# X fills spread over the eight units of a row pair, and the row end's scaled rows formed on VectorE

## The chip, the cores and the metric

The kernel runs on one core of one Trainium2 chip. The metric is the device time of one launch in microseconds: the median of the runs, 1494.32 us before the change. Engines are named as in the profile: PE is TensorE's matmul row (PEld its weight loads), DVE is VectorE, ACT is ScalarE, POOL is GpSimd, SP is SyncE, which issues the DMAs.

## What is computed

The reference is the forward pass and the whole gradient of one E-Branchformer block: x is 2 x 4000 x 144 (bfloat16, K = 5 taps), and the outputs are the block's output and the gradients by x and by seven weights.

```python
qkv = einsum('btd,de->bte', layernorm(x), w_qkv)
p = softmax(einsum('btd,bsd->bts', q, k) * D ** (-0.5))
glob = einsum('btd,de->bte', einsum('bts,bsd->btd', p, v), w_att_out)
h = gelu(einsum('btd,de->bte', layernorm(x), w_mlp_in)); u, g = h[..., :D], h[..., D:]
gc = conv over t of layernorm(g) with dw_csgu
loc = einsum('btd,de->bte', u * gc, w_mlp_out)
m = concat([glob, loc]); m = m + conv over t of m with dw_merge
out = x + einsum('btc,cd->btd', m, w_merge)
# and jax.vjp of it all for grad_out
```

## The kernel before

For each of the two batches the kernel runs a head, an attention loop and a tail; the weights' gradients are finished at the end. The change lies in the attention loop, `phase_attn`. It holds the normalised x of one batch in SBUF, as rows (`xaa`) and transposed (`xaT`, with the 16 columns over 128 apart in `XR`), and for each of 32 blocks of 128 tokens a scaled query row block `Q_t` and its backward partner `B_t`.

**Rows and units.** The loop's index i is a row of 128 queries. A row is cut into four units c2 = 0 to 3 of 1000 keys; two rows, an even and an odd one, are a pair, so a pair has eight units, which this document numbers 0 to 7 (unit 0 is c2 = 0 of the even row). `unit(i, c2)` takes four PSUM tiles, two pS and two pD, from pools of two buffers each, and issues on PE four matmuls with 16 contracted rows (L1768, called XR here) and four with 128 (L1772, called XaT). ACT makes the exponentials Pm of pS (L1777), DVE the product Sm of pD and Pm (L1778), each in two halves, with the row sums as a by-product.

**The end of a row.** `row_end(i)` adds up the sums (ld, L1792), takes the reciprocal rl (L1794), and scales: nd and Qs on POOL (L1796, L1797), nr on POOL (L1799), br on ACT (L1801). `row_end2`, called inside the next row's first unit, between its two Sm, forms Bt = Qs nd + br on DVE (L1806). Qs and Bt have four buffers, Pm and Sm three rows.

**Two products of a finished row.** SP transposes Pm and Sm by DMA (`flip`), and two rows later `yz` multiplies them with xaa, a quarter of the row's work in each unit: 16 matmuls y (L1816); in the fourth quarter ACT copies y scaled (Q_t L1821, yd L1823) and DVE adds Zn (written over B_t, L1824). y has one PSUM buffer. `xfill(pr, f)` multiplies Sm and Pm of a pair's two rows with Qs and Bt: fill f, 0 to 10, covers three blocks of 128 keys with 12 matmuls X (L1833, L1834; the last fill has 8). Even fills are added to the accumulator acc by DVE straight from PSUM (L1841), odd ones are copied by ACT (xs, L1838) and added by POOL (L1839). X has two PSUM buffers.

**The order.** The loop is written in the order in which it runs (`manual_schedule`): each engine executes its instructions in the order of the code. Each unit has two places; the table `fills` says which fill stands at (unit, place), and before, a pair's fills ran during the following pair. At each place `Q.place()` also lets steps of the local branch run (convolutions, gelu, layer norm: tiles hs, sq, a_, h_t, gp_t, dgf, jk, dWs and others), which use one PSUM buffer (ps_f) and all engines.

Of the kernel before, what the change touches and what calls it, by code (L numbers as in the profile page):

```python
# [14 lines left out]
D = 144  # L15
# [1043 lines left out]
NBK = 32  # L1059
# [659 lines left out]
def phase_attn(k, W, b, S):  # L1719
    nc, tc = k.nc, k.tc  # L1720
    NP = 3
    GW = NBK * 128
    with ExitStack() as es:
        ab = es.enter_context(tc.tile_pool(name="at_buf", bufs=1))
        sm = es.enter_context(tc.tile_pool(name="at_sm", bufs=4))
# [31 lines left out]
        def unit(i, c2):  # L1757
            g, bi = divmod(i, 4)
            QTm, BTm, QBr = jt[g]
            pb = i % NP  # L1760
            if c2 == 0:
                st["ld", i] = sm.tile([128, 2, 8], F32, tag="ld8", name="ld8")
            ld8 = st["ld", i]
            pS = [ps_s.tile([128, 512], F32, tag="S", name="pS") for h in range(2)]
            pD = [ps_d.tile([128, 512], F32, tag="D", name="pD") for h in range(2)]
            for r, o_ in enumerate((pS[0], pD[0], pS[1], pD[1])):
                rr = slice(32 * r, 32 * r + DR)
                nc.tensor.matmul(o_[:, 0:SC], QBr[rr, bi, :], S.XR[rr, c2, 0:SC], start=True, stop=False)  # L1768
            c0 = 2 * c2 * SC
            for w_, p_ in ((QTm, pS), (BTm, pD)):  # L1770
                for h in range(2):
                    nc.tensor.matmul(p_[h][:, 0:SC], w_[:, bi, :], S.xaT[:, c0 + h * SC:c0 + (h + 1) * SC], start=False, stop=True)  # L1772
            with tc.high_priority():
                for h in range(2):
                    c1 = c0 + h * SC
                    n = 2 * c2 + h
                    nc.scalar.activation(P[:, pb, c1:c1 + SC], pS[h][:, 0:SC], ACT.Exp, accum_out=ld8[:, 0, n:n + 1])  # L1777
                    nc.vector.scalar_tensor_tensor(Sm[:, pb, c1:c1 + SC], pD[h][:, 0:SC], 1.0, P[:, pb, c1:c1 + SC], op0=ALU.mult, op1=ALU.mult,  # L1778
                                                   accum_out=ld8[:, 1, n:n + 1])
# [8 lines left out]
        def row_end(i):  # L1788
            pb = i % 4
            ld8 = st.pop(("ld", i))  # L1790
            ld = sm.tile([128, 2], F32, tag="ld")
            nc.vector.reduce_sum(ld[:], ld8[:], axis=AX.X)  # L1792
            rl = sm.tile([128, 1], F32, tag="rl", bufs=6)
            nc.vector.reciprocal(rl[:], ld[:, 0:1])  # L1794
            nd = sm.tile([128, 1], F32, tag="nd", bufs=6)
            nc.gpsimd.tensor_scalar(nd[:], ld[:, 1:2], rl[:], -1.0, op0=ALU.mult, op1=ALU.mult)  # L1796
            nc.gpsimd.tensor_scalar(Qs[:, pb, :], S.Q_t[:, i, :], rl[:], 1.0, op0=ALU.mult, op1=ALU.mult)  # L1797
# [3 lines left out]
            nc.scalar.activation(br[:], S.B_t[:, i, :], ACT.Copy, scale=rl[:])  # L1801
            st["rl", i], st["nr", i], st["nd", i], st["br", i] = rl, nr, nd, br

        def row_end2(i):
            pb = i % 4
            nc.vector.scalar_tensor_tensor(Bt[:, pb, :], Qs[:, pb, :], st.pop(("nd", i))[:], st.pop(("br", i))[:], op0=ALU.mult, op1=ALU.add)  # L1806

        def yz(i, part):
            if part == 0:
# [13 lines left out]
                nc.scalar.activation(yd[:], y[:, 0, :], ACT.Copy, scale=nr[:])  # L1823
                nc.vector.scalar_tensor_tensor(S.Zn[:, i, :], y[:, 1, :], rl[:], yd[:], op0=ALU.mult, op1=ALU.add)  # L1824

        def xfill(pr, f):
            j0 = f * 3
            nj = min(3, NBK - j0)
            X = ps_x.tile([128, 3, D], F32, tag="x", name="X")
            for jj in range(nj):  # L1830
                j = j0 + jj
                for kk, i in enumerate((2 * pr, 2 * pr + 1)):
                    nc.tensor.matmul(X[:, jj, :], Sm[:, i % NP, j * 128:(j + 1) * 128], Qs[:, i % 4, :], start=(kk == 0), stop=False)  # L1833
                    nc.tensor.matmul(X[:, jj, :], P[:, i % NP, j * 128:(j + 1) * 128], Bt[:, i % 4, :], start=False, stop=(kk == 1))  # L1834
            a_ = S.acc[:, j0:j0 + nj, :]
            if f % 2 == 1:
                xs = xp.tile([128, 3, D], F32, tag="xs", name="xs")
                nc.scalar.copy(xs[:, 0:nj, :], X[:, 0:nj, :])  # L1838
                nc.gpsimd.tensor_tensor(a_, xs[:, 0:nj, :], a_, op=ALU.add)  # L1839
            else:  # L1840
                nc.vector.tensor_tensor(a_, X[:, 0:nj, :], a_, op=ALU.add)  # L1841

        fills = {(1, 0): 0, (1, 1): 1, (2, 0): 2, (2, 1): 3, (3, 0): 4, (3, 1): 5, (4, 0): 6, (4, 1): 7, (5, 1): 8, (6, 0): 9, (6, 1): 10}
        Q = Steps()
        local_steps(k, W, b, S, es, ps_f, Q)
        with tc.manual_schedule():
            for _ in jit(0):
                pass  # L1850
# [468 lines left out]
```

## Time and profile before

| What | Value |
|---|---|
| median of 3 runs | 1494.32 us (1491.7 to 1496.08) |
| the profiled execution | 1494.56 us, span 1492.7 us |
| mean granted TensorE clock | 0.936 |
| attention loop, first batch | about 84 to 606 us of the span |
| attention loop, second batch | about 782 to 1324 us of the span |

The two stretches that the prediction tabulates, 160 to 640 us and 830 to 1325 us, lie nearly wholly in these loops. In a row of the timeline stand the start (us from the span's start), the duration, the engine, the line, and in brackets how long the engine had been idle and what ended that. A row of the waits names the waiting engine and line, what it waited for, the total in us, how often, and the longest. Matmul rows overlap each other, since PE is pipelined.

### The profile page before, as it was taken

To read this page: it belongs to the slowest core of one execution; us is meant where nothing else is said; L and a number is where in the kernel's file an instruction comes from. 1 tells how busy PE (TensorE), PEld (TensorE's weight loads), DVE (VectorE), ACT (ScalarE), POOL (GpSimd) and SP (SyncE) were. 2 spreads that over 40 slices of the span, in tenths; PEclk is the share of its full clock that TensorE was granted. 3 is DMA by queue.
4 is the path that set the end of the run, shared out by engine and by line. 5 is a ranking of instruction groups with operands and counts; after the bars stand their busy time and mean duration, and the time that the engine had idled before them with its cause. 6 is when DMAs were issued, how large, how long until landed. Compare 5 with 4: busy or idle time off the path is not lost. (4 is left out here: it accounts for less than half of the span.)

```text
span 1492.7 us, 40175 instructions
## 1 busy us (share of the span) xinstructions
PE 1318.6 (88%) x15366; PEld 989.9 (66%) x15366; DVE 890.4 (60%) x3021; ACT 829.3 (56%) x2441; POOL 572.9 (38%) x1065
## 2 busy tenths in 40 slices
PE   5989999999999999889679999999999999979932
PEld 3727767776676777789553767767776677679811
DVE  5535667677666666456334577667667666635442
ACT  3746666565666665354365666666666665435310
POOL 2224435344344443355232444444434443235400
PEclk9959999999999999999895999999999999999955
DMA  5438888799888788856525997999998979867420
GB/s 139 114 73 155 157 153 161 142 171 161 146 153 169 138 166 162 180 172 178 184 76 99 158 171 128 168 162 167 162 167 151 165 142 176 161 150 205 128 92 13
DMA packets 652290, 220.67 MB, mean 148 GB/s; under 512 B 589876, under 2 KB 649012, under 8 KB 652084
## 3 DMA queue, kind: packets, MB, share of 16 engines
q1 hardware_dynamic: 651220, 217.89, 74.1%
q8 instruction: 122, 2.00, 0.6%
q14 instruction: 84, 0.69, 0.2%
q10 hardware_dynamic: 864, 0.09, 0.1%
HBM read 58.00 MB, written 25.13 MB: 56 GB/s over the span
## 5 line engine op out<-in xcount | busy, mean ns | idle before, releaser
L1778 DVE SCALAR_TENSOR_TENSOR Sm<-pD,Pm 128x500 bf16<-128x500 f32 x512 | 331.1, 675 | 290.6 <-ACT Pm L1777 230.3
L1777 ACT ACTIVATE Pm<-pS 128x500 bf16<-128x500 f32 x512 | 295.1, 583 | 128.7 <-PE pS L1772 126.4
L1839 POOL TENSOR_TENSOR acc<-xs,acc 128x432 f32<-128x432 f32 x160 | 179.9, 1124 | 395.5 <-ACT xs L1838 393.6
L1834 PE MATMUL X<-Bt,Pm 128*128 128x144 bf16 x2048 | 294.7, 228 | 1.0 <-DVE Bt L1806 1.0
L1833 PE MATMUL X<-Qs,Sm 128*128 128x144 bf16 x2048 | 294.9, 228 | 0.5 <-POOL Qs L1797 0.5
L1833 PEld LDWEIGHTS <-Sm 128*128 128x128 bf16 x2048 | 202.1, 99 | 19.3 <-issue 2.9
L1834 PEld LDWEIGHTS <-Pm 128*128 128x128 bf16 x2048 | 201.9, 99 | 19.2 <-issue 2.6
L1772 PE MATMUL pS<-xaT,QTm 128*128 128x500 bf16 x512 | 162.8, 402 | 0.0
L1772 PE MATMUL pD<-xaT,BTm 128*128 128x500 bf16 x512 | 160.7, 397 | 0.0
L1838 ACT COPY xs<-X 128x432 f32<-128x432 f32 x160 | 83.2, 520 | 138.9 <-PE X L1834 138.2
L1768 PE MATMUL pD<-XR,QBr 16*128 16x500 bf16 x512 | 132.6, 393 | 24.4 <-DVE Sm L1778 23.4
L1816 PE MATMUL y<-xaa,PT 128*128 128x144 bf16 x2048 | 152.7, 229 | 1.4 <-DVE B_t L1824 1.2
L1816 PE MATMUL y<-xaa,ST 128*128 128x144 bf16 x2048 | 149.0, 226 | 0.0
L1816 PEld LDWEIGHTS <-PT 128*128 128x128 bf16 x2048 | 137.1, 100 | 7.6 <-issue 2.0
L1841 DVE TENSOR_TENSOR acc<-X,acc 128x432 f32<-128x432 f32 x192 | 111.0, 578 | 41.8 <-PE X L1834 41.7
L1816 PEld LDWEIGHTS <-ST 128*128 128x128 bf16 x2048 | 132.9, 98 | 4.5
L1768 PE MATMUL pS<-XR,QBr 16*128 16x500 bf16 x512 | 118.6, 396 | 5.8 <-ACT Pm L1777 4.3
L1777 ACT ACTIVATION_READ_ACCUMULATOR Pm<-pS 128x1 f32 x512 | 102.7, 201 | 0.0
L1772 PEld LDWEIGHTS <-QTm 128*128 128x128 bf16 x512 | 29.4, 98 | 108.8 <-issue 108.8
L1772 PEld LDWEIGHTS <-BTm 128*128 128x128 bf16 x512 | 52.5, 103 | 65.9 <-issue 12.5
L1768 PEld LDWEIGHTS <-QBr 16*128 16x128 bf16 x1024 | 30.5, 91 | 65.6 <-issue 40.9
L2009 POOL TENSOR_SCALAR cc<-xaa,n 128x144 f32<-128x144 bf16 x64 | 35.6, 563 | 67.8 <-DVE n L2006 53.7
(584 smaller groups left out, 2600.8 us busy)
## 6 DMA issues: line engine op xcount, KB each, us to landing
gs<-in_grad_out_dram SPq DMA_DIRECT2D x24, 720.0 KB
gtap<-gn_d SPq DMA_DIRECT2D x16, 720.0 KB
dh_d<-dh SPq DMA_DIRECT2D x32, 144.0 KB
dhr<-dh_d SPq DMA_DIRECT2D x16, 288.0 KB
gs<-in_grad_out_dram SPq DMA_DIRECT2D x8, 540.0 KB
xg<-in_x_dram SPq DMA_DIRECT2D x28, 144.0 KB
dug_d<-dug SPq DMA_DIRECT2D x16, 144.0 KB
gn_d<-gn_t SPq DMA_DIRECT2D x32, 72.0 KB
```

Of the source, the lines that this page charges most:

```text
L1768: nc.tensor.matmul(o_[:, 0:SC], QBr[rr, bi, :], S.XR[rr, c2, 0:SC], start=True, stop=False)
L1772: nc.tensor.matmul(p_[h][:, 0:SC], w_[:, bi, :], S.xaT[:, c0 + h * SC:c0 + (h + 1) * SC], start=False, stop=True)
L1777: nc.scalar.activation(P[:, pb, c1:c1 + SC], pS[h][:, 0:SC], ACT.Exp, accum_out=ld8[:, 0, n:n + 1])
L1778: nc.vector.scalar_tensor_tensor(Sm[:, pb, c1:c1 + SC], pD[h][:, 0:SC], 1.0, P[:, pb, c1:c1 + SC], op0=ALU.mult, op1=ALU.mult, accum_out=l ...
L1816: nc.tensor.matmul(y[:, w, :], src[:, jj, :], S.xaa[:, j, :], start=(j == 0), stop=(j == NBK - 1))
L1833: nc.tensor.matmul(X[:, jj, :], Sm[:, i % NP, j * 128:(j + 1) * 128], Qs[:, i % 4, :], start=(kk == 0), stop=False)
L1834: nc.tensor.matmul(X[:, jj, :], P[:, i % NP, j * 128:(j + 1) * 128], Bt[:, i % 4, :], start=False, stop=(kk == 1))
L1838: nc.scalar.copy(xs[:, 0:nj, :], X[:, 0:nj, :])
L1839: nc.gpsimd.tensor_tensor(a_, xs[:, 0:nj, :], a_, op=ALU.add)
L1841: nc.vector.tensor_tensor(a_, X[:, 0:nj, :], a_, op=ALU.add)
L2009: nc.gpsimd.tensor_scalar(cc[:, q, :], S.xaa[:, 2 * p + q, :], n[:, 1, q:q + 1], n[:, 0, q:q + 1], op0=ALU.mult, op1=ALU.add)
```

## The change

The table of fills becomes one of lists: each entry names fills and which of the pair's two rows they take. Fills 2 to 10 run whole, at (unit, place) (1, 0), (1, 1), (2, 1), (3, 0), (3, 1), (4, 1), (5, 0), (5, 1), (6, 1) of the following pair. Fills 0 and 1 are split by row: the even row's half of both at unit 7 of the pair itself, the odd row's half of both at unit 0 of the following pair; their two PSUM tiles stay open in between. Within a fill the order of the matmuls is by row and no longer by key block, and only a tile's first matmul carries the start flag. `row_end` now stands right behind the row's last unit, and forms nd, Qs, br and Bt on DVE; `row_end2` is gone, nr alone stays on POOL.

```diff
-                    if c2 == 0 and h == 0 and i > 0:
-                        row_end2(i - 1)
...
-            nc.gpsimd.tensor_scalar(nd[:], ld[:, 1:2], rl[:], -1.0, op0=ALU.mult, op1=ALU.mult)
-            nc.gpsimd.tensor_scalar(Qs[:, pb, :], S.Q_t[:, i, :], rl[:], 1.0, op0=ALU.mult, op1=ALU.mult)
+            nc.vector.tensor_scalar(nd[:], ld[:, 1:2], rl[:], -1.0, op0=ALU.mult, op1=ALU.mult)
+            nc.vector.tensor_scalar(Qs[:, pb, :], S.Q_t[:, i, :], rl[:], None, op0=ALU.mult)
+            br = sm.tile([128, D], F32, tag="br", bufs=2)
+            nc.vector.tensor_scalar(br[:], S.B_t[:, i, :], rl[:], None, op0=ALU.mult)
+            nc.vector.scalar_tensor_tensor(Bt[:, pb, :], Qs[:, pb, :], nd[:], br[:], op0=ALU.mult, op1=ALU.add)
             nr = sm.tile([128, 1], F32, tag="nr", bufs=6)
             nc.gpsimd.tensor_scalar(nr[:], nd[:], rl[:], 1.0, op0=ALU.mult, op1=ALU.mult)
-            br = sm.tile([128, D], F32, tag="br", bufs=2)
-            nc.scalar.activation(br[:], S.B_t[:, i, :], ACT.Copy, scale=rl[:])
...
-        def xfill(pr, f):
+        def xfill(pr, f, rows=(0, 1)):
             j0 = f * 3
             nj = min(3, NBK - j0)
-            X = ps_x.tile([128, 3, D], F32, tag="x", name="X")
-            for jj in range(nj):
-                j = j0 + jj
-                for kk, i in enumerate((2 * pr, 2 * pr + 1)):
-                    nc.tensor.matmul(X[:, jj, :], Sm[...], Qs[:, i % 4, :], start=(kk == 0), stop=False)
-                    nc.tensor.matmul(X[:, jj, :], P[...], Bt[:, i % 4, :], start=False, stop=(kk == 1))
+            if 0 in rows:
+                st["X", f] = ps_x.tile([128, 3, D], F32, tag="x", name="X")
+            X = st["X", f]
+            for kk in rows:
+                i = 2 * pr + kk
+                for jj in range(nj):
+                    j = j0 + jj
+                    nc.tensor.matmul(X[:, jj, :], Sm[...], Qs[:, i % 4, :], start=(kk == 0 and jj == 0), stop=False, skip_group_check=True)
+                    nc.tensor.matmul(X[:, jj, :], P[...], Bt[:, i % 4, :], start=False, stop=(kk == 1), skip_group_check=True)
+            if 1 not in rows:
+                return
...
-        fills = {(1, 0): 0, (1, 1): 1, (2, 0): 2, (2, 1): 3, (3, 0): 4, (3, 1): 5, (4, 0): 6, (4, 1): 7, (5, 1): 8, (6, 0): 9, (6, 1): 10}
+        fills = {(0, 1): ((0, (1,)), (1, (1,))), (1, 0): ((2, (0, 1)),), ... (7, 1): ((0, (0,)), (1, (0,)))}
...
                         unit(i, c2)
-                    if c2 == 0 and i == NBK:
-                        row_end2(i - 1)
+                        if c2 == 3:
+                            row_end(i)
                     for place in range(2):
-                        f = fills.get((half * 4 + c2, place))
-                        if f is not None and 0 <= pr < NBK // 2:
-                            xfill(pr, f)
+                        for f, rows in fills.get((half * 4 + c2, place), ()):
+                            q = pr + 1 if rows == (0,) else pr
+                            if 0 <= q < NBK // 2:
+                                xfill(q, f, rows)
...
-                    if c2 == 3 and i < NBK:
-                        row_end(i)
```

On DVE, at the boundary of rows 11 and 12 of the second batch, from the last Sm of row 11 (its result also goes to the sums, ld with a number), there stood before:

```order
L1778 SCALAR_TENSOR_TENSOR Sm,ld_17272<-pD,Pm 128x500 x2
L1824 SCALAR_TENSOR_TENSOR B_t<-y,rl,yd 128x144
L1669 SCALAR_TENSOR_TENSOR jk,s_17498<-dgf,gn_t 128x144 x2
L1671 TENSOR_SCALAR n_17558<-s_17498 128x4
L1598 TENSOR_TENSOR a__17494<-a__17494,hs 128x576
L1700 TENSOR_TENSOR dWs<-pw,dWs 128x336
L1792 TENSOR_REDUCE ld<-ld_17272 128x2
L1794 RECIPROCAL rl<-ld 128x1
L1778 SCALAR_TENSOR_TENSOR Sm,ld_17582<-pD,Pm 128x500
L1806 SCALAR_TENSOR_TENSOR Bt<-Qs,nd,br 128x144
L1778 SCALAR_TENSOR_TENSOR Sm,ld_17582<-pD,Pm 128x500 x3
```

and at the same place stands now (the lines from L1779 on have moved by up to six):

```order
L1778 SCALAR_TENSOR_TENSOR Sm,ld_17287<-pD,Pm 128x500 x2
L1790 TENSOR_REDUCE ld<-ld_17287 128x2
L1792 RECIPROCAL rl<-ld 128x1
L1794 TENSOR_SCALAR nd<-ld,rl 128x1
L1795 TENSOR_SCALAR Qs<-Q_t,rl 128x144
L1797 TENSOR_SCALAR br<-B_t,rl 128x144
L1798 SCALAR_TENSOR_TENSOR Bt<-Qs,nd,br 128x144
L1819 SCALAR_TENSOR_TENSOR B_t<-y,rl,yd 128x144
L1669 SCALAR_TENSOR_TENSOR jk,s_17498<-dgf,gn_t 128x144 x2
L1671 TENSOR_SCALAR n_17584<-s_17498 128x4
L1598 TENSOR_TENSOR a__17494<-a__17494,hs 128x576
L1700 TENSOR_TENSOR dWs<-pw,dWs 128x336
```

The row end has moved ahead of Zn's row and the local steps, it has three instructions more, and Bt no longer stands between two Sm.

On ACT, at the same boundary, from the last exponentials of row 11 to those of row 12's first two units, there stood before:

```order
L1777 ACTIVATE Pm,ld_17272<-pS 128x500 x2
L1821 ACTIVATE Q_t<-y,rl 128x144
L1823 ACTIVATE yd<-y,nr 128x144
L1801 ACTIVATE br<-B_t,rl 128x144
L1777 ACTIVATE Pm,ld_17582<-pS 128x500 x2
L1601 ACTIVATE a__17494<-a__17494 128x576
```

and now:

```order
L1777 ACTIVATE Pm,ld_17287<-pS 128x500 x2
L1816 ACTIVATE Q_t<-y,rl 128x144
L1818 ACTIVATE yd<-y,nr 128x144
L1777 ACTIVATE Pm,ld_17597<-pS 128x500 x2
L1839 COPY xs<-X 128x432
L1601 ACTIVATE a__17494<-a__17494 128x576
```

The br ahead of the next row's exponentials is gone; the copy of fill 1 has come behind them.

On PE, at the end of row 12's first unit, the last y and what follows it, before:

```order
L1816 LDWEIGHTS PT
L1816 MATMUL y<-xaa,PT 128x144
L1768 LDWEIGHTS QBr
L1768 MATMUL pS<-XR,QBr 128x500
L1768 LDWEIGHTS QBr
```

and now, where the odd row's halves of fills 0 and 1 begin:

```order
L1811 LDWEIGHTS PT
L1811 MATMUL y<-xaa,PT 128x144
L1831 LDWEIGHTS Sm
L1831 MATMUL X<-Qs,Sm 128x144
L1832 LDWEIGHTS Pm
```

Twelve X matmuls now stand between that y and the next unit's XR.

More of the change, by code (lines that the diff above doesn't have):

```diff
@@ L1795, in row_end @@
             nd = sm.tile([128, 1], F32, tag="nd", bufs=6)
-            nc.gpsimd.tensor_scalar(nd[:], ld[:, 1:2], rl[:], -1.0, op0=ALU.mult, op1=ALU.mult)
-            nc.gpsimd.tensor_scalar(Qs[:, pb, :], S.Q_t[:, i, :], rl[:], 1.0, op0=ALU.mult, op1=ALU.mult)
+            nc.vector.tensor_scalar(nd[:], ld[:, 1:2], rl[:], -1.0, op0=ALU.mult, op1=ALU.mult)
[3 more added lines that the diff above has]
+            nc.vector.scalar_tensor_tensor(Bt[:, pb, :], Qs[:, pb, :], nd[:], br[:], op0=ALU.mult, op1=ALU.add)
             nr = sm.tile([128, 1], F32, tag="nr", bufs=6)
             nc.gpsimd.tensor_scalar(nr[:], nd[:], rl[:], 1.0, op0=ALU.mult, op1=ALU.mult)
-            br = sm.tile([128, D], F32, tag="br", bufs=2)
[L1801 to L1806, printed above, removed]
+            st["rl", i], st["nr", i] = rl, nr
         def yz(i, part):
@@ L1824, in yz @@
                 nc.vector.scalar_tensor_tensor(S.Zn[:, i, :], y[:, 1, :], rl[:], yd[:], op0=ALU.mult, op1=ALU.add)
-        def xfill(pr, f):
+        def xfill(pr, f, rows=(0, 1)):
             j0 = f * 3
             nj = min(3, NBK - j0)
-            X = ps_x.tile([128, 3, D], F32, tag="x", name="X")
-            for jj in range(nj):
-                j = j0 + jj
-                for kk, i in enumerate((2 * pr, 2 * pr + 1)):
-                    nc.tensor.matmul(X[:, jj, :], Sm[:, i % NP, j * 128:(j + 1) * 128], Qs[:, i % 4, :], start=(kk == 0), stop=False)
-                    nc.tensor.matmul(X[:, jj, :], P[:, i % NP, j * 128:(j + 1) * 128], Bt[:, i % 4, :], start=False, stop=(kk == 1))
+            if 0 in rows:
[5 more added lines that the diff above has]
+                    j = j0 + jj
+                    nc.tensor.matmul(X[:, jj, :], Sm[:, i % NP, j * 128:(j + 1) * 128], Qs[:, i % 4, :], start=(kk == 0 and jj == 0), stop=False, skip_group_check=True)
+                    nc.tensor.matmul(X[:, jj, :], P[:, i % NP, j * 128:(j + 1) * 128], Bt[:, i % 4, :], start=False, stop=(kk == 1), skip_group_check=True)
+            if 1 not in rows:
+                return
+            st.pop(("X", f))
             a_ = S.acc[:, j0:j0 + nj, :]
@@ L1841, in xfill @@
                 nc.vector.tensor_tensor(a_, X[:, 0:nj, :], a_, op=ALU.add)
-        fills = {(1, 0): 0, (1, 1): 1, (2, 0): 2, (2, 1): 3, (3, 0): 4, (3, 1): 5, (4, 0): 6, (4, 1): 7, (5, 1): 8, (6, 0): 9, (6, 1): 10}
+        fills = {(0, 1): ((0, (1,)), (1, (1,))), (1, 0): ((2, (0, 1)),), (1, 1): ((3, (0, 1)),), (2, 1): ((4, (0, 1)),), (3, 0): ((5, (0, 1)),), (3, 1): ((6, (0, 1)),),
+                 (4, 1): ((7, (0, 1)),), (5, 0): ((8, (0, 1)),), (5, 1): ((9, (0, 1)),), (6, 1): ((10, (0, 1)),), (7, 1): ((0, (0,)), (1, (0,)))}
         Q = Steps()
```

## The prediction

> **What bounds the kernel now.** I read the page's totals first, then a table of windows by stage, then the same view with one window for each unit, then the waits, and last the timelines of three engines at two row boundaries.
>
> ```profile
> PE 1318.6 (88%) x15366; PEld 989.9 (66%) x15366; DVE 890.4 (60%) x3021; ACT 829.3 (56%) x2441; POOL 572.9 (38%) x1065
> ...
> 160.00:640.00 480.00, 448.43 (x5386) 338.78 (x5383) 315.97 (x987) 288.49 (x856) 198.98 (x367) 0.98 0.86 160
> 830.00:1325.00 495.00, 466.46 (x5630) 351.74 (x5628) 332.25 (x1036) 303.46 (x904) 207.44 (x377) 0.99 0.90 159
> ```
>
> The execution took 1494.56 us, 0.24 above the median 1494.32, so the sum made against it stands for the median too. The two stretches of the attention loop (columns: time, then PE, PEld, DVE, ACT, POOL busy, clock, DMA share, GB/s) are two thirds of the span. TensorE is busy 93 to 94% of them at a granted clock of 0.98 to 0.99; no other engine exceeds 67%. So PE's stream is the bound and what can be won is its idle time: 31.6 us and 28.5 us. The next rows say where it sits. Each is the sum line of a windows view whose windows run from the first XR matmul (L1768) of a unit to that of the next, over rows 2 to 31 of both batches: unit 0 (the first quarter of an even row) to unit 7 (the last of an odd one), 30 windows each, 28 for unit 7.
>
> ```profile
> sum 111.79, PE 95.24 PEld 59.05 DVE 69.31 ACT 77.86 POOL 48.60; mean PE 3.17 PEld 1.97 DVE 2.31 ACT 2.60 POOL 1.62
> sum 160.47, PE 147.08 PEld 105.94 DVE 111.28 ACT 73.37 POOL 40.78; mean PE 4.90 PEld 3.53 DVE 3.71 ACT 2.45 POOL 1.36
> sum 132.86, PE 131.01 PEld 104.63 DVE 79.93 ACT 76.63 POOL 49.18; mean PE 4.37 PEld 3.49 DVE 2.66 ACT 2.55 POOL 1.64
> sum 128.92, PE 128.92 PEld 104.01 DVE 75.96 ACT 100.37 POOL 56.73; mean PE 4.30 PEld 3.47 DVE 2.53 ACT 3.35 POOL 1.89
> sum 130.44, PE 124.38 PEld 97.61 DVE 91.13 ACT 81.51 POOL 77.14; mean PE 4.15 PEld 3.25 DVE 3.04 ACT 2.72 POOL 2.57
> sum 119.45, PE 110.86 PEld 79.89 DVE 88.18 ACT 74.93 POOL 55.97; mean PE 3.70 PEld 2.66 DVE 2.94 ACT 2.50 POOL 1.87
> sum 127.22, PE 123.14 PEld 92.87 DVE 96.22 ACT 79.85 POOL 49.60; mean PE 4.10 PEld 3.10 DVE 3.21 ACT 2.66 POOL 1.65
> sum 78.69, PE 76.49 PEld 52.98 DVE 53.14 ACT 56.12 POOL 35.12; mean PE 2.73 PEld 1.89 DVE 1.90 ACT 2.00 POOL 1.25
> ```
>
> Time less PE busy is 16.6, 13.4, 1.9, 0, 6.1, 8.6, 4.1 and 2.2 us: 52.7 us in all, 29.9 of it in units 0 and 1. Units 2 and 3, which hold two X fills each and follow units with two, have almost none; units 0 and 7 hold no fill, unit 5 one. A unit's XR matmuls write pS and pD, two buffers each, so they wait for Exp (ACT) and Sm (DVE) of the unit before; y, X and the local steps on PE cover that wait. Who is late, and why, shows in the waits and at the boundary of rows 11 and 12 of the second batch:
>
> ```profile
> ACT br L1801 <- DVE rl L1794: 57.3, 42, 2.4
> PE pD L1768 <- DVE Sm L1778: 23.4, 62, 1.6
> ```
> ```profile
> 968.81 0.38 PE L1768 MATMUL pS<-XR,QBr 16*128 16x500 bf16 x1
> ...
> 970.02 1.16 PE L1816 MATMUL y<-xaa,PT 128*128 128x144 bf16 x16
> 972.28 0.37 PE L1768 MATMUL pS<-XR,QBr 16*128 16x500 bf16 x1 [1.10 <-ACT Pm L1777]
> ...
> 973.88 0.37 PE L1768 MATMUL pD<-XR,QBr 16*128 16x500 bf16 x1 [0.49 <-DVE Sm L1778]
> ```
> ```profile
> 968.12 0.68 DVE L1778 SCALAR_TENSOR_TENSOR Sm<-pD,Pm 128x500 bf16<-128x500 f32 x1
> 968.72 0.08 DVE L1778 DVE_READ_ACCUMULATOR Sm<-pD,Pm 128x1 f32 x1
> 969.02 0.37 DVE L1824 SCALAR_TENSOR_TENSOR B_t<-y,rl,yd 128x144 bf16<-128x144 f32 x1 [0.21 <-ACT yd L1823]
> ...
> 970.45 0.50 DVE L1700 TENSOR_TENSOR dWs<-pw,dWs 128x336 f32<-128x336 f32 x1
> 970.86 0.16 DVE L1792 TENSOR_REDUCE ld<-ld 128x2 f32<-128x16 f32 x1
> 971.06 0.16 DVE L1794 RECIPROCAL rl<-ld 128x1 f32<-128x1 f32 x1
> 972.27 0.68 DVE L1778 SCALAR_TENSOR_TENSOR Sm<-pD,Pm 128x500 bf16<-128x500 f32 x1 [1.05 <-ACT Pm L1777]
> ...
> 973.15 0.67 DVE L1778 SCALAR_TENSOR_TENSOR Sm<-pD,Pm 128x500 bf16<-128x500 f32 x1
> ```
> ```profile
> 968.34 0.38 ACT L1821 ACTIVATE Q_t<-y,rl 128x144 bf16<-128x144 f32 x1 [0.28 <-PE y L1816]
> 968.62 0.37 ACT L1823 ACTIVATE yd<-y,nr 128x144 f32<-128x144 f32 x1
> 971.25 0.41 ACT L1801 ACTIVATE br<-B_t,rl 128x144 f32<-128x144 bf16 x1 [2.27 <-DVE rl L1794]
> 971.58 0.57 ACT L1777 ACTIVATE Pm<-pS 128x500 bf16<-128x500 f32 x1
> ```
>
> The last Sm of row 11 ends at 968.80, yet rl comes at 971.06, behind Zn's row (L1824) and local work. br stands on ACT ahead of the next row's Exp and holds it until 971.58, then Bt splits the two Sm by 0.88 us, and PE, done with y at 971.18, gets its last XR in at 973.88. PE has nothing else to do: unit 0 has no fill.
>
> **The change, part by part.**
>
> *X fills.* All 4096 X matmuls stay; a fill's 12 are the same form as y's 16, which take (1.16 - 0.23) / 15 = 0.062 us each, so a fill is 0.75 us. Units 0 to 7 held 0, 2, 2, 2, 2, 1, 2, 0 fills (the last of the 11 is short) and get 1, 2, 1, 2, 1, 2, 1, 1. 0.75 us goes into unit 0 and its 1.0 us mean of idle time with unit 1, where it costs nothing. In unit 7 only 0.1 us of it is covered at once; units 2, 4 and 6 become shorter by as much.
>
> *br, nd and Qs to DVE.* ACT loses 64 br, and Exp no longer queues behind rl. A light boundary, rows 7 and 8, shows what that is worth:
>
> ```profile
> 905.83 0.16 DVE L1794 RECIPROCAL rl<-ld 128x1 f32<-128x1 f32 x1
> 906.35 0.57 ACT L1777 ACTIVATE Pm<-pS 128x500 bf16<-128x500 f32 x1
> 906.30 1.16 PE L1816 MATMUL y<-xaa,PT 128*128 128x144 bf16 x16
> 908.66 0.37 PE L1768 MATMUL pD<-XR,QBr 16*128 16x500 bf16 x1 [0.49 <-DVE Sm L1778]
> ```
>
> There the Exp starts 0.52 us after rl; freed of it and of Bt between the Sm, the XR could come 0.8 us sooner, at 907.9; PE ends y at 907.46 and with its new fill gets there at 908.2, so PE is the later one and the whole stall goes. At rows 11 and 12 DVE is the later one. From 968.80 it has ld and rl (0.4 by the two starts above), nd, Qs, br and Bt, together 1.4 us by the prices below, then Zn's row and 1.5 us of local work: about 972.0 for the first Sm instead of 972.27, and 0.28 us less between the two. The XR group ends 0.55 us sooner with 0.75 us more work done, which is half of the stall there (the last XR came 2.7 us after the end of y; its rows overlap each other and hide part of that from the idle times).
>
> The prices of nd, Qs and br on DVE are not in the trace. The nearest rows:
>
> ```profile
> L1797 POOL TENSOR_SCALAR Qs<-Q_t,rl x64: 382/387/393, 98.1 to 1307.5; 128x144 bf16<-128x144 bf16 x64
> L1671 DVE TENSOR_SCALAR n<-s x32: 169/170/1575, 210.5 to 1309.2; 128x4 f32<-128x4 f32 x32
> L1806 DVE SCALAR_TENSOR_TENSOR Bt<-Qs,nd,br x64: 361/365/785, 100.1 to 1308.2; 128x144 bf16<-128x144 bf16 x64
> L1839 POOL TENSOR_TENSOR acc<-xs,acc x160: 1093/1102/1369, 120.6 to 1321.8; 128x432 f32<-128x432 f32 x160
> ```
>
> Below, L1671's 0.17 us each; above, Bt's 0.365, the same width with two tensors read. I take 0.17, 0.2 and 0.3, because one input is less than Bt's two: 0.7 us, ld to Bt 1.4 us. Undisturbed that fits the 1.05 us of DVE idle time before the next Sm and the wait for yd that it now fills. The maxima warn: a DVE row of 0.17 us has taken 1.575, Bt 0.785, and a POOL add 1.369 instead of 1.10. DVE and POOL sometimes hold each other up. At an odd fill ACT copies and POOL adds; fill 5 moves to the first place of unit 3, so its POOL add of 1.1 us comes about when the last Sm of that unit ends, on top of the new chain. Between 0 and 1.1 us for each of 32 such boundaries, 35 us at most; I take 0.5 us, half of it hidden by unit 4's cover: 8 us.
>
> The page "SBUF — State Buffer" of the Trainium skill ("Who interferes with whom") says that a DVE instruction in a two-port mode, or with two SBUF inputs, and a GpSimd instruction that reads SBUF exclude each other for a whole instruction; the maxima above agree. By it Qs, br and Bt could each meet POOL's add, and the sum would lose up to those 35 us instead of 8.
>
> *Row end ahead of Zn.* Zn's row now starts after Bt, and y's one PSUM bank is free later. Between y's last matmul of unit 7 and the next y stand 0.75 us of X and 1.2 us of XR and XaT (968.81 to 970.02); from the start of ACT's two copies to the end of Zn's row passed 1.05 us (968.34 to 969.39). The chain's 1.4 us puts Zn's end at about 970.5, and PE with its fill at 970.8. From 0 to 0.3 us a row, I take 0.05: 3 us.
>
> *X buffers.*
>
> ```profile
> L1841 DVE TENSOR_TENSOR acc<-X,acc 128x432 f32<-128x432 f32 x192 | 111.0, 578 | 41.8 <-PE X L1834 41.7
> ```
>
> Fills 0 and 1 hold both X buffers over the boundary. Fill 2 heads unit 1's X work and waits for DVE's add of fill 0, which stands behind unit 0's Sm and local steps. That add takes 0.58 us, against the 1.2 us of XR and XaT in front of fill 2: from 0 to 1 us a pair, I take 0.1: 3 us.
>
> POOL loses nd and Qs; the yd that reads nr comes two rows later. SP's flips stay where they are in its queue.
>
> *Sum.* Units 0 and 1: 29.9 us shown idle, all of it in light rows and half in heavy ones, so about three quarters, and XR rows hide a little more: -25. Unit 7: -2. Units 4 to 6, 18.8 us: the same block by br leaves unit 4, unit 5 gets a fill, but 4 and 6 lose one: a third, -6. The pair's end is one half fill shorter in each batch: -1. New waits 8 + 3 + 3, less 5 that slack of the shorter units takes: +9. 1494.6 - 34 + 9 = 1469.6, which I give as 1469.
>
> **Rivals.**
> - *Nearly all idle time goes.* If POOL is seldom in the way, the chain is short and balanced units cover what is left: 52.7 us shown and some hidden under XR rows: 1494.6 - 55 = 1440. For it: units 2 and 3. Against: in heavy rows DVE itself is late.
> - *DVE takes ACT's place.* With POOL's add in the new chain at every second boundary (the 35 us), Sm is late by as much as br held it, and units 4 and 6 with one fill no longer cover it: 1469 + 35 - 8 - 5 = 1491. For it: the maxima above; DVE's 111 us of 160 in unit 1. This is the mechanism that the page's rule would make regular.
> - *Slower, by the X buffers.* Fill 2 stands at the head of PE's queue in unit 1; behind it wait y and the next XR. If DVE's local steps between unit 0's Sm and its add of fill 0 take as long as the 1.5 us at rows 11 and 12, in every pair, fill 2 is about 1 us late in each of 32: 1469 - 3 + 32 = 1498. It decides from 0.9 us a pair. Against: XR of unit 1 waits for the same Sm, so PE is late with it.
>
> **How the numbers follow.** Forecast 0.58, all idle time 0.20, DVE in ACT's place 0.14, X buffers 0.08. Range 1438 to 1489: the gain's upper end is the idle time shown, the lower is the DVE rival. A measurement tells about 0.3% (4.5 us) from no change. Faster: the first two, and the better half of the third, 0.85. Same: the rest of it, 0.07. Slower: 0.08.
>
> **What would show it.** Right: the wait of ACT at br is gone; PE's wait pD <- Sm falls from 23.4 us to under 10; the window sums of units 0 and 1 shrink together by little while units 2, 4 and 6 lose 0.7 us each; DVE goes from Sm to Bt in 1.2 to 1.6 us. Wrong: nd, Qs or br far over 0.3 us in the mean, a wait of X on DVE's add, or idle time on PE in units 4 and 6 above 10 us each.

## The result, and the profile after

The changed kernel takes 1451.68 us (median of 4 runs, 1451.34 to 1455.19), the kernel before 1493.01 beside it (4 runs, 1490.24 to 1496.08): a ratio of 0.9728, 95% interval 0.9702 to 0.9754. It is 2.7% faster, 41 us where 25 were forecast; the time lies inside the range of 1438 to 1489. Ratios here compare runs of one session on one chip and leave disturbed runs out, so they differ a little from the quotient of two medians. The profiled execution has a span of 1449.8 us against 1492.7, 42.9 less. First the totals of its page and, from the same page's costliest groups, the two groups of XR matmuls (busy us, mean ns | idle us before them, and what ended it):

```profile
PE 1289.7 (89%) x15366; PEld 981.9 (68%) x15366; DVE 933.5 (64%) x3213; ACT 807.8 (56%) x2377; POOL 544.5 (38%) x937
...
L1768 PE MATMUL pD<-XR,QBr 16*128 16x500 bf16 x512 | 119.2, 393 | 4.6 <-DVE Sm L1778 4.2
L1768 PE MATMUL pS<-XR,QBr 16*128 16x500 bf16 x512 | 110.6, 395 | 1.7 <-ACT QBr L1755 1.4
```

The same two groups on the page of before:

```profile
L1768 PE MATMUL pD<-XR,QBr 16*128 16x500 bf16 x512 | 132.6, 393 | 24.4 <-DVE Sm L1778 23.4
L1768 PE MATMUL pS<-XR,QBr 16*128 16x500 bf16 x512 | 118.6, 396 | 5.8 <-ACT Pm L1777 4.3
```

The idle time in front of XR is mostly gone (30.2 us to 6.3), as forecast. But PE's busy time fell too, by 28.9 us, with the same 15366 matmuls, at the same mean per XR row (393 to 396 ns); 21.4 us of that fall are XR's. One XR row takes as long as before, so what changed is how the rows overlap. Before, at the boundary of rows 11 and 12, unit 0's four XR started within 0.05 us of each other and ran side by side (968.81 to 968.86). Unit 1's four got their buffers one after the other and started at three times from 972.28 to 973.88, and each time counts as 0.37 us busy of its own. Two of these rows, beside those that the prediction shows:

```profile
968.86 0.37 PE L1768 MATMUL pD<-XR,QBr 16*128 16x500 bf16 x1
...
973.01 0.37 PE L1768 MATMUL pD<-XR,QBr 16*128 16x500 bf16 x1 [0.36 <-DVE Sm L1778]
```

So before, a part of XR's stall stood in the profile as busy time. In the 60 windows of units 0 and 1 that are tabulated below, the time from the first to the last XR start of a unit adds up to 37.3 us before and to 2.4 now. The clock has hardly a part in it: in two stretches of the attention loops it was granted at 0.99, as before at 0.98 and 0.99 (a windows view, columns as in the prediction):

```profile
158.60:614.00 455.40, 432.25 (x5352) 333.06 (x5350) 331.99 (x1068) 278.44 (x828) 185.62 (x310) 0.99 0.92 169
830.00:1289.00 459.00, 434.84 (x5383) 334.04 (x5381) 335.09 (x1073) 281.11 (x833) 184.82 (x309) 0.99 0.92 166
```

Where the time came from shows in the windows by unit, cut as in the prediction (units 0 to 7, rows 2 to 31 of both batches):

```profile
sum 116.39, PE 107.26 PEld 78.48 DVE 98.64 ACT 64.78 POOL 50.21; mean PE 3.58 PEld 2.62 DVE 3.29 ACT 2.16 POOL 1.67
sum 130.88, PE 125.17 PEld 98.65 DVE 92.24 ACT 76.84 POOL 66.15; mean PE 4.17 PEld 3.29 DVE 3.07 ACT 2.56 POOL 2.20
sum 111.05, PE 107.56 PEld 81.08 DVE 74.22 ACT 71.03 POOL 51.65; mean PE 3.59 PEld 2.70 DVE 2.47 ACT 2.37 POOL 1.72
sum 128.95, PE 128.95 PEld 104.03 DVE 100.73 ACT 97.64 POOL 36.13; mean PE 4.30 PEld 3.47 DVE 3.36 ACT 3.25 POOL 1.20
sum 109.90, PE 102.52 PEld 74.96 DVE 100.01 ACT 69.89 POOL 44.66; mean PE 3.42 PEld 2.50 DVE 3.33 ACT 2.33 POOL 1.49
sum 139.69, PE 135.61 PEld 103.96 DVE 97.64 ACT 75.13 POOL 65.73; mean PE 4.52 PEld 3.47 DVE 3.25 ACT 2.50 POOL 2.19
sum 100.20, PE 96.42 PEld 69.86 DVE 61.62 ACT 71.74 POOL 55.27; mean PE 3.21 PEld 2.33 DVE 2.05 ACT 2.39 POOL 1.84
sum 102.03, PE 98.62 PEld 73.91 DVE 75.65 ACT 71.69 POOL 17.46; mean PE 3.52 PEld 2.64 DVE 2.70 ACT 2.56 POOL 0.62
```

A unit's change in time less the X work that it gained or lost (0.75 us a fill; 30 windows, 28 for unit 7) is the change of its stalls:

| Units | before | after | change | X work | stalls |
|---|---|---|---|---|---|
| 0 and 1 | 272.26 | 247.27 | -25.0 | +22.5 | -47.5 |
| 2 and 3 | 261.78 | 240.00 | -21.8 | -22.5 | +0.7 |
| 4 | 130.44 | 109.90 | -20.5 | -22.5 | +2.0 |
| 5 | 119.45 | 139.69 | +20.2 | +22.5 | -2.3 |
| 6 | 127.22 | 100.20 | -27.0 | -22.5 | -4.5 |
| 7 | 78.69 | 102.03 | +23.3 | +21.0 | +2.3 |
| all | 989.84 | 939.09 | -50.8 | -1.5 | -49.3 |

Outside these windows 7.9 us were lost, which makes -42.9: by the first and last bounds of the windows, the first row 2 starts 1.5 us later, the stretch from the last whole pair of batch 1 to row 2 of batch 2 takes 5.8 us more, and what follows the last window 0.6. Of these 7.9 us 1.5 are X work that moved there (rows 0 and 1 of each batch gained a fill's time). The 5.8 are 1.5 in the end of batch 1's last pair (from the start of its unit 7 to the end of its last X 19.75 us before, 21.24 now), 1.2 in batch 2's first two rows (26.45 to 27.62, with that X in them), and 3.1 in the code between, which the change leaves alone and which took 2.4 us less in a second profile of the changed kernel. In units 0 and 1, PE's time that shows as idle fell from 29.9 us to 14.8, by 15.1. The other 32.4 of the 47.5 us are busy time that went although there was more to do (242.32 us busy before, 232.43 now, with 22.5 us of X added): stall hidden under rows that count as busy.

The boundary of rows 11 and 12 in the second batch, DVE's timeline, and then the last XR of row 12's units 0 and 1 on PE:

```profile
937.65 0.08 DVE L1778 DVE_READ_ACCUMULATOR Sm<-pD,Pm 128x1 f32 x1
937.77 0.17 DVE L1790 TENSOR_REDUCE ld<-ld 128x2 f32<-128x16 f32 x1
938.17 0.21 DVE L1794 TENSOR_SCALAR nd<-ld,rl 128x1 f32<-128x1 f32 x1
938.30 0.25 DVE L1795 TENSOR_SCALAR Qs<-Q_t,rl 128x144 bf16<-128x144 bf16 x1
938.46 0.29 DVE L1797 TENSOR_SCALAR br<-B_t,rl 128x144 f32<-128x144 bf16 x1
938.79 0.37 DVE L1798 SCALAR_TENSOR_TENSOR Bt<-Qs,nd,br 128x144 bf16<-128x144 bf16 x1
...
940.91 0.67 DVE L1778 SCALAR_TENSOR_TENSOR Sm<-pD,Pm 128x500 bf16<-128x500 f32 x1
```
```profile
938.50 0.38 PE L1768 MATMUL pD<-XR,QBr 16*128 16x500 bf16 x1
...
942.24 0.37 PE L1768 MATMUL pD<-XR,QBr 16*128 16x500 bf16 x1 [0.21 <-DVE Sm L1778]
```

The chain from ld to the end of Bt takes 1.39 us here (forecast 1.4), and the first Sm starts 3.18 us after the end of the last one (937.73; forecast 3.2). The last XR of unit 1 starts 4.51 us after the end of that Sm, before 5.08 us (968.80 to 973.88): 0.57 us sooner with 0.75 us more work done, where the prediction had 0.55. PE's own step shows more. From the last XR of unit 0 to the last of unit 1 pass 3.74 us with a fill in it, before 5.02 us (968.86 to 973.88), so 2.0 us of stall went between them, not the 1.3 that the prediction counted. Unit 0's XR come 0.7 us later after that Sm than before, behind the X work that now stands in unit 7, and PE has that much less to wait for in unit 1.

Three waits of the changed kernel (total us, times, longest):

```profile
PE y L1811 <- DVE B_t L1819: 8.9, 22, 1.0
PE X L1831 <- DVE acc L1842: 4.4, 4, 2.1
PE pD L1768 <- DVE Sm L1778: 4.2, 18, 0.4
```

The first two are the forecast's new waits. A third cost is in no such row. In the even rows the chain is mostly not 1.4 us long. Timelines of DVE and POOL at the end of row 10, second batch, and DVE's group of Bt over the whole run (min/median/max in ns):

```profile
922.08 1.24 DVE L1798 SCALAR_TENSOR_TENSOR Bt<-Qs,nd,br 128x144 bf16<-128x144 bf16 x1
922.06 1.10 POOL L1840 TENSOR_TENSOR acc<-xs,acc 128x432 f32<-128x432 f32 x1
```
```profile
L1798 DVE SCALAR_TENSOR_TENSOR Bt<-Qs,nd,br x64: 367/399/1321, 98.8 to 1264.5; 128x144 bf16<-128x144 bf16 x64
```

Bt of 0.37 us takes 1.23 to 1.32 us in 26 of the 32 even rows (the expectations below say 27, one too many), each time with POOL's add of fill 5 starting within 0.06 us of Bt and running for 1.07 to 1.10 us of it. In two more even rows Bt keeps its 0.37 us, and the add takes 1.27. It is no accident of timing: on POOL that add stands right behind nr (L1800), and nr waits for nd and starts 0.3 us ahead of Bt, so the chain itself lets POOL start when Bt is about to.

### The profile page after: what moved, and what is told of

It reads as the page before. It is cut to its first block, busy times and chain, and to the rows that moved or that the text cites. A ratio compares the mean times of both kernels' runs of the same rounds, so it can differ in the third digit from the quotient of the medians.

```text
span 1449.8 us, 40173 instructions
## 1 busy us (share of the span) xinstructions
PE 1289.7 (89%) x15366; PEld 981.9 (68%) x15366; DVE 933.5 (64%) x3213; ACT 807.8 (56%) x2377; POOL 544.5 (38%) x937
## 5 line engine op out<-in xcount | busy, mean ns | idle before, releaser
L1778 DVE SCALAR_TENSOR_TENSOR Sm<-pD,Pm 128x500 bf16<-128x500 f32 x512 | 326.3, 675 | 226.6 <-ACT Pm L1777 185.4
L1811 PE MATMUL y<-xaa,PT 128*128 128x144 bf16 x2048 | 149.4, 226 | 9.1 <-DVE B_t L1819 8.9
L1772 PE MATMUL pD<-xaT,BTm 128*128 128x500 bf16 x512 | 157.5, 390 | 0.0
L1768 PE MATMUL pD<-XR,QBr 16*128 16x500 bf16 x512 | 119.2, 393 | 4.6 <-DVE Sm L1778 4.2
L1800 POOL TENSOR_SCALAR nr<-nd,rl 128x1 f32<-128x1 f32 x64 | 22.6, 353 | 258.5 <-DVE nd L1794 258.5
L1768 PE MATMUL pS<-XR,QBr 16*128 16x500 bf16 x512 | 110.6, 395 | 1.7 <-ACT QBr L1755 1.4
```

Source lines behind the costliest of these rows:

```text
L1811: nc.tensor.matmul(y[:, w, :], src[:, jj, :], S.xaa[:, j, :], start=(j == 0), stop=(j == NBK - 1))
```

## The experiments

Four kernels first, each the kernel before with one part of the change; their median of before is 1491.8 us. My theory was that ACT's queue is the cause: br stands at its head, waits for rl, and holds the next row's exponentials. The rivals gave the gain to the balance of the fills, or to the place of the row end.

**Fills alone** (the row end as before):

```diff
-        fills = {(1, 0): 0, (1, 1): 1, (2, 0): 2, ...}
+        fills = {(0, 1): ((0, (1,)), (1, (1,))), (1, 0): ((2, (0, 1)),), ... (7, 1): ((0, (0,)), (1, (0,)))}
```

> Before, with the fills of the changed kernel and the row end as it was (nd, Qs on POOL, br on ACT behind the whole last unit, Bt between the next row's two Sm). Queue theory (br on ACT held the next row's Exp, and this is the larger half of the loss): Exp still waits in unit 0, the new work there hides part of it, but unit 4 has lost a fill and shows the same wait bare: about 15 us faster than before, ACT's wait at br stays near 57 us. Cover theory (PE only lacked work in units 0, 7 and 5): 35 us or more faster, nearly all of the change's 41.

Measured: 1468.1 us, ratio 0.9833 (0.9794 to 0.9873). Its waits:

```profile
ACT br L1801 <- DVE rl L1794: 64.7, 50, 2.6
...
PE X L1837 <- DVE Bt L1806: 15.8, 22, 1.1
```

ACT still waits at br, more than before (57.3 us), yet the fills alone win 1.7%, 25 us, between the 15 and the 35 that the two theories gave: X work now stands where PE waited, and part of the stall became a wait of X for Bt.

**The row end alone** (nd, Qs, br and Bt on DVE, early; the old fills): the other hunks of the diff.

> Before, with the new row end alone (all of nd, Qs, br, Bt on DVE right behind the last unit), fills as they were. Queue theory: about 25 us faster; the wait pD <- Sm falls from 23.4 us to about 10, what is left is unit 0 without work. Cover theory: under 10 us faster, since unit 0 and unit 7 still hold no fill and PE idles there as before.

Measured: 1464.53 us, 0.9806 (0.9762 to 0.9849). Its waits:

```profile
PE y L1811 <- DVE B_t L1819: 12.9, 22, 1.3
...
PE pD L1768 <- DVE Sm L1778: 6.9, 23, 0.7
```

1.9%, with no X in unit 0 to cover y's wait for Zn.

**br alone on DVE**, at its late place:

```diff
-            nc.scalar.activation(br[:], S.B_t[:, i, :], ACT.Copy, scale=rl[:])
+            nc.vector.tensor_scalar(br[:], S.B_t[:, i, :], rl[:], None, op0=ALU.mult)
```

> Before, with one instruction moved: br on DVE instead of ACT, at its old place behind the whole last unit; nd and Qs stay on POOL, Bt stays between the two Sm, fills as they were. Queue theory: the Exp of units 0 and 4 no longer stands behind rl, so most of what the row end alone gives comes from this one move: 12 to 20 us faster. Rival (what matters is that the whole row end comes early on DVE, ahead of Zn and the local steps): 0 to 6 us, because Bt now waits for POOL's Qs between the two Sm as before and DVE still reaches rl late.

Measured: 1457.84 us, 0.9775 (0.9732 to 0.9819). Its windows of units 0 and 1:

```profile
sum 100.17, PE 92.12 PEld 57.10 DVE 82.56 ACT 77.27 POOL 44.53; mean PE 3.07 PEld 1.90 DVE 2.75 ACT 2.58 POOL 1.48
sum 144.79, PE 133.88 PEld 99.06 DVE 103.66 ACT 64.10 POOL 46.87; mean PE 4.46 PEld 3.30 DVE 3.46 ACT 2.14 POOL 1.56
```

One instruction on another engine gives 34 us, more than the 12 to 20 I expected and no less than the whole new row end (the intervals overlap). Units 0 and 1 lose 27.3 us (272.26 to 244.96) with not a matmul moved. ACT's queue was the larger cause.

**The place alone**: `row_end` right behind the last unit, every instruction on its old engine.

```diff
                         unit(i, c2)
+                        if c2 == 3:
+                            row_end(i)
...
-                    if c2 == 3 and i < NBK:
-                        row_end(i)
```

> Before, with the place alone changed: the row end right behind the last unit, but nd and Qs on POOL, br on ACT and Bt between the next two Sm as they were. Queue theory: ACT's wait at br is now for rl right behind the last Sm, and Exp of the next row comes later anyway, so this too frees the Exp: 12 to 20 us faster, but ACT's copies of y stand behind br now. Rival (the engine matters, not the place): 0 to 5 us.

Measured: 1501.36 us, 1.0046 (1.002 to 1.0072): slower, which neither theory expected. Two of its waits, and its window of unit 7:

```profile
ACT br L1801 <- DVE rl L1794: 79.0, 64, 2.1
...
PE y L1816 <- DVE B_t L1824: 8.7, 12, 1.4
```
```profile
sum 91.09, PE 76.94 PEld 53.05 DVE 57.93 ACT 55.77 POOL 40.28; mean PE 2.75 PEld 1.89 DVE 2.07 ACT 1.99 POOL 1.44
```

An earlier rl doesn't help an engine that stops for it earlier. Here br waits for rl in all 64 rows, and ahead of more: ACT's copies of y and the local steps of that unit stand behind it, y waits for Zn's row, and unit 7 grew from 78.69 to 91.09 us. My theory held as to who waits, but had not asked what else stands in that queue.

Four more, beside a median of before of 1491.5 us, cross the parts.

**br on DVE and the new fills** (the first and third edits together):

> The new fills and, of the row end, only br moved to DVE at its old late place; nd and Qs on POOL, Bt between the next row's two Sm. Theory now (ACT's queue behind br was the larger part, and br alone off ACT gave 34 us; the new fills need Bt early): X in unit 0 waits for Bt, which comes after the first Sm, as in the kernel with the fills alone (15.8 us of wait there), a little less because Exp is sooner: about 8 us of wait, 36 to 42 us faster than before. Rival (an early row end is needed for the new fills): X <- Bt stays at 15 us or more, no faster than br alone, 30 to 34 us.

Measured: 1443.03 us, 0.9662 (0.9641 to 0.9684), faster than the changed kernel and, with 48 us, than the 36 to 42 I expected. Its waits:

```profile
PE pD L1768 <- DVE Sm L1778: 5.1, 18, 0.5
...
PE X L1836 <- POOL Qs L1797: 2.2, 6, 0.5
PE X L1837 <- DVE Bt L1806: 2.2, 12, 0.2
...
PE y L1816 <- DVE B_t L1824: 1.8, 4, 0.6
```

With br's 2.25% and the fills' 1.67% the two would give 3.92% if they didn't overlap; they give 3.38%, which is within the noise of the three ratios. nd and Qs on POOL, and Bt between two Sm, cost PE almost nothing once ACT is free.

**The change with the row end back at its late place** (all four rows on DVE):

```diff
-                        if c2 == 3:
-                            row_end(i)
...
+                    if c2 == 3 and i < NBK:
+                        row_end(i)
```

> The changed kernel with row_end at its old place, behind the whole last unit; all of it still on DVE, new fills. Theory now (the early place costs: y waits 8.9 us for Zn, which stands behind the new chain): the wait y <- B_t (Zn) falls to about 1 us, X <- Bt appears with 3 to 6 us in the heavy rows; within 4 us of the changed kernel, 38 to 45 us faster than before. Rival (the early place is what makes the change): 28 us faster or less.

Measured: 1445.91 us, 0.9689 (0.9671 to 0.9708), about 46 us where 38 to 45 were expected. Two of its waits:

```profile
PE pD L1768 <- DVE Sm L1778: 7.2, 28, 0.6
...
PE y L1811 <- DVE B_t L1819: 2.0, 4, 0.6
```

**All four rows on DVE, late, with the old fills:**

> The old fills, row_end all on DVE at its old late place. It lies between the new row end alone (all on DVE, early, 27 us faster) and br alone (late, 34 us faster). If the early place is what makes the first slower than the second: 33 to 38 us faster, the wait y <- Zn gone (12.9 us in the first). If the extra DVE work of nd, Qs and Bt in one piece does it: 26 to 29 us.

Measured: 1468.65 us, 0.9845 (0.9824 to 0.9865): 23 us, less than either expectation. Its window of unit 1:

```profile
sum 155.28, PE 143.23 PEld 102.87 DVE 109.74 ACT 63.66 POOL 39.53; mean PE 4.77 PEld 3.43 DVE 3.66 ACT 2.12 POOL 1.32
```

With the old fills, nd, Qs and Bt on DVE ahead of the next row's first Sm take back 10.5 us of br's gain in unit 1 alone (144.79 with br only). A part of that can be POOL again: Qs, 0.25 us elsewhere, takes 0.57 to 1.07 us in 10 of 64 places here, each time beside one of POOL's adds.

**The row end behind Zn's row, ahead of the rest of the last unit:**

```diff
-                        if c2 == 3:
-                            row_end(i)
...
+                        if place == 0 and c2 == 3 and i < NBK:
+                            row_end(i)
```

> The changed kernel with row_end behind the first place of the last unit, that is behind Zn and that place's local steps, but ahead of the second place's. Theory now: Zn no longer waits for the chain (y <- Zn from 8.9 to about 1 us), Bt is still ready when unit 0's fills come, so X <- Bt stays under 2 us: 3 to 8 us faster than the changed kernel, 44 to 49 faster than before. Rival (Zn's wait for ACT's yd now holds back the chain, and Sm of the next row with it): 36 to 41 us faster than before, no better than the changed kernel.

Measured: 1452.97 us, 0.9724 (0.9699 to 0.9749): 38 us, not the 44 and more that I expected of it. The profiled execution was the slowest of its six (1459.06 us). Waits and the window of unit 5:

```profile
DVE B_t L1819 <- ACT yd L1818: 34.3, 39, 1.8
...
PE pD L1768 <- DVE Sm L1778: 8.8, 33, 1.1
...
PE y L1811 <- DVE B_t L1819: 1.7, 4, 0.6
```
```profile
sum 149.93, PE 142.18 PEld 105.19 DVE 111.35 ACT 76.35 POOL 67.88; mean PE 4.74 PEld 3.51 DVE 3.71 ACT 2.55 POOL 2.26
```

y's wait for Zn falls from 8.9 us to 1.7, and the time stays: it comes back as the wait for Sm, with unit 5 at 149.93 us against 139.69 and unit 1 at 137.38 against 130.88. That is the rival of the expectation: Zn's row waits for yd (34.3 us, 6.9 in the changed kernel), and the chain stands behind it. Bt is hardly held here either (392 ns in the mean of 64), so this kernel has neither y's wait nor the hold that the changed kernel has, and a new cost in their place; it prices neither. Gains in per cent of before, by fills and row end, show what is left to explain:

| | row end as before | br on DVE, late | all on DVE, late | all on DVE, early |
|---|---|---|---|---|
| old fills | 0 | 2.25 | 1.55 | 1.94 |
| new fills | 1.67 | 3.38 | 3.11 | 2.72 |

Only with the new fills does the early place lose against the late one, and only there does POOL's add of fill 5 meet Bt: Bt's mean over 64 is 376 ns with the old fills and the early place, 416 ns with the new fills and the late place, and 741 ns in the changed kernel. The last kernels test that.

**Fill 5 added by DVE, fill 6 by ACT and POOL** (beside this and the next two kernels before has a median of 1490.9 us):

```diff
-            if f % 2 == 1:
+            if f in (1, 3, 6, 7, 9):
```

> The changed kernel with fills 5 and 6 exchanged in who evacuates them: fill 5 is added by DVE straight from PSUM, fill 6 is copied by ACT and added by POOL. In the changed kernel Bt took 1.24 to 1.32 us instead of 0.37 in 27 of 32 even rows, each time while POOL's add of fill 5 ran. If POOL's add is what holds Bt: Bt is back at 0.37 us in the even rows and the chain ld to Bt at 1.4 us; DVE's sum falls by 20 us or more, and 3 to 8 us of it reach the time, since most of the delay hid behind unit 4's cover. If it is something else (the weight of DVE's own queue there, SBUF traffic of PE or DMA): Bt stays over 1 us, same time within 2 us.

Measured: 1455.75 us, 0.9768 (0.9741 to 0.9795). Bt, and the wait of y:

```profile
L1798 DVE SCALAR_TENSOR_TENSOR Bt<-Qs,nd,br x64: 367/368/399, 99.2 to 1264.4; 128x144 bf16<-128x144 bf16 x64
```
```profile
PE y L1811 <- DVE B_t L1819: 11.1, 20, 1.3
```

The hold is gone, yet no time is won: DVE now does that add itself, and it comes ahead of Zn's row. The run says that the collision needs POOL's add, but not what it costs.

**nd, Qs and nr early on POOL, br and Bt on DVE between the next row's two Sm:**

```diff
         def row_end2(i):
             pb = i % 4
+            br = sm.tile([128, D], F32, tag="br", bufs=2)
+            nc.vector.tensor_scalar(br[:], S.B_t[:, i, :], st["rl", i][:], None, op0=ALU.mult)
...
```

> The new fills with the row end in two parts: ld and rl on DVE right behind the last unit, nd, Qs and nr on POOL, nothing on ACT; br and Bt on DVE between the next row's two Sm. It takes the early rl without putting more than 0.35 us ahead of Zn. Against the fills with br on DVE, late (48.5 us faster): Qs and nd are ready sooner, so the waits X <- Qs and X <- Bt (4.4 us there) go: 48 to 53 us faster than before. If br between the two Sm delays the second Sm as much as it relieves: 44 to 48.

Measured: 1444.41 us, 0.9688 (0.9664 to 0.9713): as good as the late places, 46 us and so the lesser of the two expected gains, with 11.7 us of X waiting for the late Bt. **The changed kernel once more**, on the same chip:

> The changed kernel itself, unedited, beside the other two on the same chip: 38 to 43 us faster than before.

Measured: 1451.15 us, 0.9737 (0.9711 to 0.9763).

**POOL held back**: a small POOL instruction that reads Bt into a scratch column that nothing uses stands behind nr in even rows, so that fill 5's add starts after Bt. Nothing else changes (before: 1491.2 us).

```diff
             nc.gpsimd.tensor_scalar(nr[:], nd[:], rl[:], 1.0, op0=ALU.mult, op1=ALU.mult)
+            if i % 2 == 0:
+                dm = sm.tile([128, 1], F32, tag="dm", bufs=1)
+                nc.gpsimd.tensor_scalar(dm[:], Bt[:, pb, 0:1], 1.0, 0.0, op0=ALU.mult, op1=ALU.add)
```

> The changed kernel with one small POOL instruction more, behind nr in the even rows, which reads one column of Bt into a scrap tile: POOL's add of fill 5 stands behind it and so starts after Bt. DVE, ACT and PE keep their instructions and order. If POOL's add is what holds Bt, Bt is back at 0.37 us in the even rows. In time, if that hold reaches PE (the chain 0.9 us shorter in 27 of 32 rows, y's wait for Zn in unit 4 of 3.8 us gone): 3 to 8 us faster than the changed kernel. If it is covered by unit 4's slack, or DVE's next instructions with two inputs meet the add instead: within 2 us of the changed kernel, whose ratio to before is 0.973.

Measured: 1439.54 us, 0.9663 (0.9629 to 0.9698), the fastest median here. Bt and the new instruction, y's wait, and the windows of units 4 and 5:

```profile
L1798 DVE SCALAR_TENSOR_TENSOR Bt<-Qs,nd,br x64: 367/368/397, 98.8 to 1249.1; 128x144 bf16<-128x144 bf16 x64
...
L1803 POOL TENSOR_SCALAR dm<-Bt x32: 191/191/338, 99.2 to 1232.5; 128x1 f32<-128x1 bf16 x32
```
```profile
PE y L1814 <- DVE B_t L1822: 7.5, 16, 1.0
```
```profile
sum 108.09, PE 101.71 PEld 74.91 DVE 92.10 ACT 69.83 POOL 61.08; mean PE 3.39 PEld 2.50 DVE 3.07 ACT 2.33 POOL 2.04
sum 133.22, PE 131.77 PEld 102.27 DVE 91.46 ACT 74.99 POOL 64.25; mean PE 4.39 PEld 3.41 DVE 3.05 ACT 2.50 POOL 2.14
```

Work was added on POOL, and the kernel is faster by 0.65 to 0.74% (against the changed kernel's two ratios), some 10 us where 3 to 8 were expected; the intervals leave about 3 to 17. Bt's rows are some 24 us shorter in sum, DVE's whole busy time only 15.7 (933.5 to 917.8), so other DVE rows took a part of it back. Units 4 and 5, behind the even row's end, give 8.3 us of the gain (1.8 and 6.5). Here the early place is as good as the late one (0.9663 against 0.9689, intervals overlapping), though y still waits 7.5 us for Zn: y's wait is not what the early place had lost.

## Why the prediction was right and where it was wrong

**Right.** The direction and the mechanism: br on ACT waited for rl and held the exponentials; br alone moved wins 34 us. PE's wait pD <- Sm went from 23.4 us to 4.2 (forecast: under 10). The prices of nd, Qs and br (0.17, 0.2, 0.3) measured 0.214, 0.248 and 0.290 us in the mean, 0.75 together against 0.7. The undisturbed chain took 1.39 us against 1.4, and the heavy boundary, counted from the last Sm, came out as worked out. Units 2, 4 and 6 lose 0.73, 0.68 and 0.90 us each (forecast 0.7). Units 4 to 6 gave 4.8 us of stall against 6.

**The step that failed is the term for units 0 and 1, -25.** It counted what the windows showed as idle, 29.9 us, took three quarters, and added "a little more" for what XR rows hide. The stalls that went there are 47.5 us: 15.1 that showed as idle and 32.4 that showed as busy. The sign that the prediction gave, that these two windows "shrink together by little", failed by the same amount: they shrank by 25.0 us, with 22.5 us of X added. The cure was in the prediction's own rows: at rows 11 and 12 it read 2.7 us between the end of y and the last XR, of which 1.95 show as idle in front of XR (1.10, 0.36 and 0.49), but carried the shown idle time into the sum. And it let half of that stall go, 1.3 us, where 2.0 went on PE. The missing 22.5 us are more than the forecast's whole error of 18 (1469.6 forecast against the profiled execution's 1451.7); that the error is not larger is luck, since other terms erred the other way. Against the sum, the other units came out 6.2 us worse (0.7 for units 2 and 3, 1.2 for 4 to 6, 4.3 for 7) and what lies outside the windows 7.4 (6.4 of stall where 1 was to be won), while the 9 us for new waits are already in these figures: 22.5 - 6.2 - 7.4 + 9 = 17.9.

**The new waits** were sized too low, which covers a part of that. POOL's hold was put at 8 us and measured about 10. The forecast had it as 0.5 us at each of 32 boundaries, half of it hidden; it is 0.91 us more per Bt in 26 of them, 24 us on DVE (47.4 us for all 64 Bt, 23.7 with POOL held back), of which something under half reaches the end. y for Zn shows 8.9 us against 3, and X for DVE's add 4.4 against 3, though y's wait is worth little by itself, as the kernel with POOL held back shows. Unit 7 lost 2.3 us where 2 were to be won. The end of the last pair, put at 1 us of gain in all, lost 1.5 us in each batch, and the other losses outside the windows were not in the sum.

**The rivals.** "Nearly all idle time goes" (1440) came nearest: 12 us away, the forecast 18. Its condition, POOL seldom in the way, was not met, and the kernel that meets it takes 1439.5 us, with other terms off as well. "DVE takes ACT's place" had the mechanism and too high a price: units 4 and 5 bear the hold at 8.3 us, since part of it is covered. Its rule, from the page "SBUF — State Buffer" of the Trainium skill, "Who interferes with whom", is that a DVE instruction with two SBUF inputs and a GpSimd instruction that reads SBUF exclude each other for a whole instruction. The traces agree for Bt, 0.37 us alone and 1.23 to 1.32 beside POOL's add. Qs and br, which the prediction feared for too, kept 0.25 and 0.29 us in all 64 rows, since they end before the add begins; in the kernel with br alone, br took 0.46 to 1.24 us in 12 of 64 places beside such an add. The X buffers' rival is out: its wait was 4.4 us in 4 places, not 1 us in each of 32.

**Still open.** Whether the gains of fills and br overlap at all, and why the end of the last pair takes 1.5 us longer in each batch, was not taken apart, nor how much of br's 34 us is its wait for rl and how much its own 0.41 us ahead of the exponentials. Whether the kernel with br alone and the new fills (0.9662) or the one with POOL held back (0.9663) is faster can't be told from these runs; both beat the changed kernel.

## What to carry to other kernels

Before moving work, read what stands at the head of an in-order engine's queue and what it waits for: here one instruction, put on an engine where its input is at hand, won 34 us by itself, where the whole change won 41. Size a stall by a stage's time against the time of its work, not by the idle time shown, where rows that can run side by side are held apart. When a chain moves to VectorE, look at what GpSimd starts on the same signal; a min/median/max row with a far maximum shows a collision, and a small dependent instruction ahead of GpSimd's long one can be worth its cost.

## What was not expected of the hardware

A DVE instruction of 0.37 us took 1.23 to 1.32 us in 26 of 32 places beside a POOL add that itself kept its 1.10 us, and a 0.19 us POOL instruction that delays the add ended that: Bt's maximum fell from 1321 to 397 ns. And PE's busy time fell by 28.9 us with the same number of matmuls and the same mean per XR row: rows that could run side by side, and are held apart, each count as busy.
